# Seven block products in place of eight in the third layer's first product, with its weights streamed from DRAM

## Chip, cores and metric

The kernel runs on 1 core of a Trainium2 chip. The metric is device microseconds of one execution. Three runs of the kernel before took 900.82, 898.17 and 900.29 us; the median is 900.29.

## What is computed

A causal linear attention with a decay per head (batch 4, 8 heads, 768 positions, head size 64) gives 3,072 tokens of 512 features. A first MLP (512 to 1,024 to 512) weights h with its softmax and normalizes it between its two products; a second MLP (512 to 2,048 to 512) puts h cos(h) between its own. Three layers are spoken of: attention; the first MLP, whose products are the first and second layer's; and the second MLP, called the third layer here.

```
x = attention(q, k, v)                      # 3072 x 512
h = x @ w_in;  solu = h * softmax(h);  x = layernorm(solu) * g_ln @ w_out
h = x @ w_in2                               # 512 -> 2048
out = (h * cos(h)) @ w_out2                 # 2048 -> 512
```

All weights are given in float64. Every product is made of three float32r passes: high by high, low by high and high by low.

## The kernel before, in words

Nothing is written in program order. `record` (L843) calls methods that hand operations to `Plan` with an engine, a cost, what they read and write, and a due time (the TensorE clock at that point plus a bias). `Plan.order` (L129) then simulates the engines: TensorE takes its list in order (with a small look ahead), the others the ready operation with the lowest due time, SyncE its transfers by due time. The order found is what is issued, so on the chip each engine works through a fixed list.

**Up to about 120 us**: w_in and w_out are turned from float64 words into float32 halves, and attention (`attn`, L337) runs five steps of 128 tokens ahead of the first layer (`mm1`, L513, then `norm`, L535).

**From 120 to 320 us**: the loop of `record` runs the last 14 steps of `mm1` and 19 of the 24 units of the second layer (`mm2`, L606: one block of 512 tokens by 128 features, 24 matmuls, y stored to DRAM) behind their transposes (`transp`, L584). Beside each unit one `keep` (L482) is handed over, 16 in all: `words` (L400) loads 1 MB of w_in2 or w_out2 as raw words (one ScalarE operation L410, four VectorE operations L414 to L430), and the float32 values go back to DRAM. Keeps alternate between two raw tiles and two word tiles.

**The seam, 320 to 384 us**: the last held unit (HOLD = 1), the transposes and `mm2` of block 5, and the first four columns of the third layer's block 0. `load_kept` (L491) brings each kept piece back once, splits it into halves on ScalarE (L502) and VectorE (L506), and leaves all of w_in2 and w_out2 in SBUF. `load_y` (L638) brings y back and splits it.

**The third layer, 384 us to the end**: for each of 6 blocks of 512 tokens, 16 columns. `up` (L714) makes one 128x512 tile of h with 12 matmuls of 128x512 (L728), over all four slices of the depth. The wave behind it is eight operations: reduction of the angle (L733 on ScalarE, L738, L742 and L746 on VectorE), sine (L749, ScalarE), product (L752, VectorE), high half (L756, ScalarE) and low half (L760, VectorE). `down` (L777) makes 12 matmuls (L789) of a finished column, three columns later, into four accumulators, which are copied and stored at the end of the block.

Of the kernel before, what the change touches and what calls it, by code (L numbers as in the profile page):

```python
# [35 lines left out]
LAG = 3  # L36
EARLY = 5
HOLD = 1
NU = 10
RING = 5  # L40
# [12 lines left out]
SHARE = 0.7  # L53
# [5 lines left out]
LAND = 2.0  # L59
LOOK = 10  # L60
# [9 lines left out]
B_YS = 6.0  # L70
B_LOAD = 4.0
B_LOW = 4.0
JOIN = 2
PARTS = ((0,), (1,), (2, 3), (0, 1), (0, 1, 2, 3))
# [23 lines left out]
class Plan:  # L98
# [30 lines left out]
    def order(self):  # L129
# [18 lines left out]
        at, sat, out, owed = 0, 0, [], 0.0  # L148
# [4 lines left out]
        while len(out) < n:  # L153
            best = None
            for e in engines:
# [6 lines left out]
                elif e == "SP":  # L162
                    while sat < len(sp) and done[sp[sat]]:
                        sat += 1
                    if sat == len(sp):
                        continue
                    cand = [i for i in sp[sat:sat + 8 + stuck] if not left[i] and not done[i]
                            and (stuck or ops[i][7] <= ops[sp[sat]][7] + SP_WIN)]
                else:
                    cand = avail[e]  # L170
# [19 lines left out]
            if e == "POOL" and ops[i][6] == "big":  # L190
                if free["DVE"] > start:
                    free["DVE"] += SHARE
                else:
                    owed = end
            if e == "DVE" and start < owed:
                end += SHARE
                owed = 0.0
# [18 lines left out]
class Body:  # L216
# [21 lines left out]
    def shut(self, name):  # L238
# [4 lines left out]
            "ltl": "lt", "o1h": "o1", "o1l": "o1", "yh": "sb", "yl": "sb", "gh": "sb",  # L243
            "gl": "sb", "h2": "psh", "acc": "psacc", "o": "wo"}

    def add(self, eng, cost, fn, r=(), w=(), **k):
        pools = set()
        for key in (*r, *w):
            if key[0] in ("raw", "wt"):
                pools.add(key[1])  # L250
            elif key[0] == "h":
                pools.add(("ps1", "psb")[key[1]])
            elif key[0] in self.home:
                pools.add(self.home[key[0]])
# [132 lines left out]
    def split(self, n):  # L387
# [9 lines left out]
        self.add("DVE", 0.70, low, r=[("x", n % RING), ("xh", n % 2)], w=[("xl", n % 2)])  # L397


    def words(self, key, src, pool, slot, apart, wide=2, late=0.0):  # L400
# [3 lines left out]
        def fetch():  # L404
            raw = self.new(pool, ("raw", key), [128, wide, 512, 2], I32, f"raw{slot}")
            self.nc.sync.dma_start(out=raw, in_=src)

        def top():
            t = self.new(pool, ("wt", key), [128, wide, 512], I32, f"wt{slot % 2}")
# [26 lines left out]
        self.add("SP", 0.5, fetch, r=[("pool", pool)], w=[rk], mb=0.5245 * wide, bias=b)  # L436
        self.add("ACT", 0.1 + 0.53 * wide, top, r=[rk], w=[wk], bias=b)
        self.add("DVE", 0.17 + 0.28 * wide, clamp, w=[wk], bias=b)
        self.add("DVE", 0.17 + 0.28 * wide, shift, w=[wk], bias=b)
        self.add("DVE", 0.15 + 0.55 * wide, sign, r=[rk], w=[wk], bias=b)  # L440
        self.add("DVE", 0.15 + 0.55 * wide, low, r=[wk] if apart else [rk], w=[rk] if apart else [wk], bias=b + late)
# [5 lines left out]
    def w1(self, c, k, wide, slot):  # L447
# [4 lines left out]
        ks = slice(k, k + wide)  # L452

        def high():
            self.nc.scalar.activation(out=self.w1h[:, ks, cs], in_=self.t["head", key], func=AF.Copy)

        def low():
            self.nc.vector.tensor_tensor(out=self.w1l[:, ks, cs], in0=self.t["full", key],
                                         in1=self.w1h[:, ks, cs].bitcast(F32), op=ALU.subtract)
# [3 lines left out]
                 bias=self.bias + B_LOW)  # L463

    def o1(self, e, pool, slot):
        key = ("o1", e)
        rk, wk = self.words(key, self.pair("w_out1", 2 * e, slice(0, 1024)), pool, slot, True)
        for i in range(2):
# [11 lines left out]
            self.add("DVE", 0.75, low, r=[rk, ("o1h", j)], w=[("o1l", j)], bias=self.bias)  # L480

    def keep(self, what, src, slot):  # L482
        rk, wk = self.words(what, src, "stg", slot, False)

        def store():
            t = self.p["dram"].tile([128, 2, 512], F32, name="kept_%s_%d_%d" % what)
            self.t["kept", what] = t
            self.nc.sync.dma_start(out=t, in_=self.t["full", what])
        self.add("SP", 0.4, store, r=[wk], w=[("kept", what)], mb=0.524, bias=self.bias + B_STORE)

    def load_kept(self, what, dst, keys, pools):  # L491

        sl = self.used["kt"] = self.used.get("kt", -1) + 1
        sl %= 2

        def fetch():
            t = self.new("stg", ("back", what), [128, 2, 512], F32, f"wt{sl}")
            self.nc.sync.dma_start(out=t, in_=self.t["kept", what])

        def high():  # L500
            hi, lo = dst()
            self.nc.scalar.activation(out=hi, in_=self.t["back", what], func=AF.Copy)  # L502

        def low():
            hi, lo = dst(False)
            self.nc.vector.tensor_tensor(out=lo, in0=self.t["back", what], in1=hi.bitcast(F32), op=ALU.subtract)  # L506
        wk = ("wt", "stg", sl)
        self.add("SP", 0.4, fetch, r=[("kept", what)], w=[wk], mb=0.524, bias=-12.0)
        self.add("ACT", 1.10, high, r=[wk] + [("pool", p) for p in pools], w=keys, bias=B_BACK)
        self.add("DVE", 1.25, low, r=[wk], w=keys, bias=B_BACK)  # L510


    def mm1(self, n, c, parts=((0, 1, 2, 3),), passes=(0, 3), look=1, done=True):  # L513
# [4 lines left out]
        for ks in parts:  # L518
            def go(ks=ks):
# [4 lines left out]
                for k in ks:  # L524
                    for m, (a, w) in list(enumerate(((xh, self.w1h), (xl, self.w1h), (xh, self.w1l))))[slice(*passes)]:
                        self.nc.tensor.matmul(out=h[:, c], lhsT=a[:, k], rhs=w[:, k, cs], start=(k + m == 0),  # L526
# [79 lines left out]
    def mm2(self, g, d, look=1):  # L606
        ds = slice(d * 128, (d + 1) * 128)
        pool = "ps1" if g == NBLK - 1 and d % 2 else "pst"
        yk = [("y1",)] if pool == "pst" else [("h", 0, 0), ("h", 0, 1)]
        for f in range(4):  # L610
# [14 lines left out]

        def copy():
# [11 lines left out]
    def load_y(self, n):  # L638
        for k in range(KD):
            def fetch(k=k):  # L640
                self.t["yt", n, k] = t = self.t["yts"][:, k]
                self.nc.sync.dma_start(out=t, in_=self.t["y1d", n][:, k])

            def high(k=k):
                if k == 0:
                    self.new("sb", ("yh", n), [128, KD, 512], F32R, "yh")
                    self.new("sb", ("yl", n), [128, KD, 512], F32R, "yl")
                self.nc.scalar.activation(out=self.t["yh", n][:, k], in_=self.t["yt", n, k], func=AF.Copy)

            def low(k=k):  # L650
                self.nc.vector.tensor_tensor(out=self.t["yl", n][:, k], in0=self.t["yt", n, k],
                                             in1=self.t["yh", n][:, k].bitcast(F32), op=ALU.subtract)
            self.add("SP", 0.4, fetch, r=[("y1d", n, k)], w=[("yt", k)], mb=0.262, bias=-15.0)
            self.add("ACT", 0.65, high, r=[("yt", k)], w=[("yh", k)] + ([("yh", i) for i in range(1, KD)] if k == 0 else []))
            self.add("DVE", 0.70, low, r=[("yt", k), ("yh", k)], w=[("yl", k)])

    def w2(self, c, e):
        what = ("in", c, e)
        ks = slice(2 * e, 2 * e + 2)
        T = self.t  # L660
        if c == 0:
            i, j = self.used["u"], self.used["u"] + 1
            self.used["u"] += 2
            keys = [("u", i % NU), ("u", j % NU)]

            def dst(fresh=True):
                if fresh:
# [392 lines left out]
```

## Time and profile before

| | |
|---|---|
| median of 3 runs | 900.29 us |
| the profiled execution | 902.23 us, span 900.2 us |
| granted TensorE clock, mean | 0.993 |
| TensorE / VectorE / ScalarE busy | 98 / 64 / 46% |
| HBM read, written | 68.2 MB, 21.0 MB |

The span is the time from the first to the last instruction; about 2 us of the execution lie around it. Durations are those of one profiled execution. Matmuls are pipelined, so one lasts longer in a row than the distance to the next; that distance is read from the chain of waits, where a run of matmuls stands with its length and count.

### The profile page before, as it was taken

How to read it: one execution, taken by the hardware profiler on the slowest of the kernel's cores; microseconds unless marked ns; L12 is line 12 of the kernel's file. 1: busy time of each engine (PE TensorE's matmuls, PEld its weight loads, DVE VectorE, ACT ScalarE, POOL GpSimd, SP SyncE). 2: the span in 40 equal slices, each digit the busy share in tenths (PEclk: the TensorE clock that was granted, in tenths of full speed). 3: DMA queues.
4: the chain of work that ended last, by engine and by line, in shares of the span. 5: the costliest groups of instructions: out<-in, count | busy, mean ns of one | idle time of the engine just before them, and what ended most of it. 6: DMA issues, size and time to landing. Idle time of an engine off the chain costs nothing.

```text
span 900.2 us, 15838 instructions
## 1 busy us (share of the span) xinstructions
PE 879.1 (98%) x6648; PEld 728.1 (81%) x6648; DVE 577.6 (64%) x849; ACT 417.0 (46%) x658; POOL 93.1 (10%) x193
## 2 busy tenths in 40 slices
PE   7899999999999999999999999999999999999997
PEld 6688888888788877878888888888888888888886
DVE  6778786867676674466566566656665565557553
ACT  4677674635445475344343343434433443334332
POOL 0134431322422220000000000000000000000000
PEclk8999999999999999999999999999999999999999
DMA  9754727666663643241030003000300030001002
GB/s 351 256 179 146 266 90 256 219 248 239 213 216 135 194 169 94 82 137 40 1 93 1 1 1 94 0 1 1 94 0 1 1 94 1 0 17 31 1 0 48
DMA packets 29031, 90.21 MB, mean 100 GB/s; under 512 B 3360, under 2 KB 3360, under 8 KB 28960
## 3 DMA queue, kind: packets, MB, share of 16 engines
q1 hardware_dynamic: 28816, 89.14, 29.9%
q8 instruction: 52, 0.85, 0.4%
q14 instruction: 19, 0.16, 0.1%
q10 hardware_dynamic: 144, 0.06, 0.0%
HBM read 68.22 MB, written 20.97 MB: 99 GB/s over the span
## 4 chain that ended last, share of the span: by engine, by line
PE 85%; DMA 7%; DVE 2%; ACT 2%; issue 2%; POOL 1%; SPq 1%; ACTq 0%; DVEq 0%; POOLq 0%
PE acc L789 29%; PE h L728 29%; PE h L526 11%; PE y L620 8%; DMA raw<-w_out_dram 2%; PE sc L313 2%; PE tr L588 2%; DMA raw<-w_in_dram 2%; DMA dk<-kq_dram 2%; PE S L321 1%; PE h L620 1%; PE y L334 1%; DMA sv<-vk_dram 1%; DMA yts<-y1d 1%; DVE wt L423 1%
## 5 line engine op out<-in xcount | busy, mean ns | idle before, releaser
L789 PE MATMUL acc<-o2h,gh 128*128 128x512 f32 x384 | 149.5, 389 | 0.7 <-ACT ys L628 0.7
L728 PE MATMUL h<-yh,w2h 128*128 128x512 f32 x384 | 149.8, 390 | 0.0
L728 PE MATMUL h<-yl,w2h 128*128 128x512 f32 x384 | 149.4, 389 | 0.0
L789 PE MATMUL acc<-o2l,gh 128*128 128x512 f32 x384 | 149.4, 389 | 0.0
L728 PE MATMUL h<-yh,w2l 128*128 128x512 f32 x384 | 149.4, 389 | 0.0
L789 PE MATMUL acc<-o2h,gl 128*128 128x512 f32 x384 | 149.4, 389 | 0.0
L749 ACT ACTIVATE kr<-kr,hp 128x512 f32<-128x512 f32 x96 | 69.4, 723 | 151.2 <-DVE kr L746 151.2
L752 DVE TENSOR_TENSOR kr<-kr,h 128x512 f32<-128x512 f32 x96 | 65.9, 686 | 62.3 <-ACT kr L749 62.3
L738 DVE SCALAR_TENSOR_TENSOR kr<-kr,h 128x512 f32<-128x512 int32 x96 | 65.8, 686 | 59.7 <-ACT kr L733 59.7
L760 DVE TENSOR_TENSOR gl<-kr,gh 128x512 fp32r<-128x512 f32 x96 | 66.3, 691 | 52.5 <-ACT gh L756 52.5
L733 ACT ACTIVATE kr<-h 128x512 int32<-128x512 f32 x96 | 57.2, 596 | 79.9 <-PE h L728 79.8
L756 ACT ACTIVATE gh<-kr 128x512 fp32r<-128x512 f32 x96 | 60.6, 631 | 61.5 <-DVE kr L752 61.4
L789 PEld LDWEIGHTS acc<-o2h,gh 128*128 128x128 f32 x384 | 72.1, 188 | 16.1 <-ACT ys L628 1.2
L728 PEld LDWEIGHTS h<-yl,w2h 128*128 128x128 f32 x384 | 72.1, 188 | 15.0
L789 PEld LDWEIGHTS acc<-o2l,gh 128*128 128x128 f32 x384 | 72.1, 188 | 15.0
L728 PEld LDWEIGHTS h<-yh,w2l 128*128 128x128 f32 x384 | 72.1, 188 | 14.9
L789 PEld LDWEIGHTS acc<-o2h,gl 128*128 128x128 f32 x384 | 72.1, 188 | 14.9
L728 PEld LDWEIGHTS h<-yh,w2h 128*128 128x128 f32 x384 | 72.0, 188 | 14.8
L526 PE MATMUL h<-w1h,xh 128*128 128x512 f32 x192 | 79.1, 412 | 1.7 <-ACT xh L390 1.7
L526 PE MATMUL h<-w1h,xl 128*128 128x512 f32 x192 | 76.2, 397 | 0.6 <-DVE xl L394 0.6
L526 PE MATMUL h<-w1l,xh 128*128 128x512 f32 x192 | 74.2, 394 | 0.1
L620 PE MATMUL y<-lth,o1h 128*128 128x512 f32 x176 | 69.9, 397 | 3.1 <-ACT ys L628 3.1
(82 smaller groups left out, 1388.3 us busy)
## 6 DMA issues: line engine op xcount, KB each, us to landing
sv<-vk_dram SPq DMA_DIRECT2D x24, 640.0 KB, 6.4
dk<-kq_dram SPq DMA_DIRECT2D x24, 512.0 KB, 6.1
raw<-w_out_dram SPq DMA_DIRECT2D x12, 1024.0 KB, 7.2
raw<-w_in_dram SPq DMA_DIRECT2D x11, 1024.0 KB, 10.0
y1d<-ys SPq DMA_DIRECT2D x24, 256.0 KB, 3.0
yts<-y1d SPq DMA_DIRECT2D x24, 256.0 KB, 4.2
out_dram<-o SPq DMA_DIRECT2D x48, 128.0 KB, 2.3
kept_in<-wt SPq DMA_DIRECT2D x8, 512.0 KB, 3.0
```

The lines of the kernel that those rows point to most:

```text
L313: self.nc.tensor.matmul(out=sc[r, j], lhsT=dk[r, 0, j], rhs=dk[r, 1, j], start=True, stop=True)
L526: self.nc.tensor.matmul(out=h[:, c], lhsT=a[:, k], rhs=w[:, k, cs], start=(k + m == 0), stop=(k == KD - 1 and m == 2))
L588: self.nc.tensor.transpose(out=tr[:, t * 128:(t + 1) * 128], in_=self.t["u", 4 * g + t].rearrange("p c f -> p (c f)")[:, j * 128:(j + 1) * ...
L620: self.nc.tensor.matmul(out=self.t["y1", g, d], lhsT=w[:, j, ds], rhs=a, start=(j + m == 0), stop=(j == K1 - 1 and m == 2))
L728: nc.tensor.matmul(out=h, lhsT=w[:, cs], rhs=a[:, k], start=(m == 0), stop=(m == 3 * KD - 1))
L733: nc.scalar.activation(out=T["ki", n, j], in_=T["h2", n, j], func=AF.Identity, scale=INV2PI, bias=0.25)
L738: nc.vector.scalar_tensor_tensor(out=r, in0=ki, scalar=-C1, in1=T["h2", n, j], op0=ALU.mult, op1=ALU.add)
L749: nc.scalar.activation(out=T["r", n, j], in_=T["r", n, j], func=AF.Sin, bias=self.hp[:, 0:1])
L752: nc.vector.tensor_tensor(out=T["r", n, j], in0=T["r", n, j], in1=T["h2", n, j], op=ALU.mult)
L756: nc.scalar.activation(out=T["gh", n, j], in_=T["r", n, j], func=AF.Copy)
L760: nc.vector.tensor_tensor(out=T["gl", n, j], in0=T["r", n, j], in1=T["gh", n, j].bitcast(F32), op=ALU.subtract)
L789: nc.tensor.matmul(out=T["acc", n, t], lhsT=a[:, ts_], rhs=w, start=(j == 0 and m == 0), stop=(j == K2 - 1 and m == 2))
```

## The change

The first product of the third layer takes 1,024 tokens (two blocks) at a time, a super-block, of which there are three. An iteration makes 256 columns of h for both blocks: a product of two by two blocks (halves of the columns, halves of the depth, the two token blocks). It is done with seven block products instead of eight, each of 6 matmuls (two slices of the depth, three passes), on sums and differences of the blocks.

- The sums and differences of w_in2 (seven slots, each as high and low half) are made in `keep`, beside the words, and stored in DRAM (`cbd`); w_out2's two halves likewise (`o2d`). There is one raw tile, one word tile and one tile `big`, through which all 16 pieces pass.
- The third layer streams them: `load_cb` brings the 1.84 MB of an iteration into one of three buffers, three iterations ahead, and `load_o2` 1.05 MB into one of three. Buffer 0 of the first is the tile `big`. The split of whole weights (`load_kept`) is gone.
- `load_y` makes the sums and differences of y for two blocks, with halves, in tiles where w_in's halves and attention's tiles stood. Half of it for the first super-block is made in the loop of the middle stage (at step 21), half after it.
- The products accumulate in banks X (two, alternating), W and Z. X is copied by ScalarE after products 1, 6 and 7, while it goes on accumulating; VectorE adds the copies to W or Z. The tiles from 2 and 4 belong to the first block of the two (near), those from 7 and 3 to the second (far).
- In the first half of a super-block the near tiles go through `parts` (what `down` was), three matmuls at a time, between the products. The far tiles wait in SBUF as finished products; in the second half their halves are made and their `parts` run, with no products beside them.
- The seam has the products of iteration 0 between the transposes and the last second-layer units; HOLD is 2, and RING, the ring of attention outputs, 4.
- The planner counts GpSimd's large operations and VectorE's operations with two inputs in SBUF as excluding each other.

```
 NBLK = NT // 512
-LAG = 3
+NSUP = NT // 1024
 EARLY = 5
-HOLD = 1
+HOLD = 2
 NU = 10
...
+ORDER = (("1", 0), ("5", 0), ("6", 0), ("2", 0), ("7", 2), ("4", 3), ("3", 3))
+SEAM = ("t:0 t:1 P:1 P:2 t:2 t:3 P:5 t:4 t:5 P:6 m:0:0:1 t:6 t:7 P:7 m:0:1:3 P:4 m:0:3:4 P:3"
+        " m:1:0:4 m:2:0:4 m:3:0:4")
...
@@ keep @@
+        rk, wk = self.words(what, src, "stg", 0, False, early=EARLIER)
...
+        def part(m, i, n, ca, cd, src):
+            self.add("ACT", ca, high(i, n, src), r=[wk], w=[("big", m)] + ([] if m else [("big",), ("big", 1), ("big", 2)]), bias=b)
+            self.add("DVE", cd, low(i, n, src), r=[wk], w=[("big", m)], bias=b, name="two")
+
+        part(0, 0, 2, 0.62, 0.70, lambda: top2(0))
+        part(1, 2, 1, 0.38, 0.42, lambda: quarter(1, 1))
+        mix((1, 1), (0, 1), (1, 1), ALU.add)
+        mix((0, 1), (0, 0), (0, 1), ALU.subtract)
+        mix((0, 0), (1, 1), (0, 0), ALU.subtract)
+        mix((1, 0), (1, 0), (0, 0), ALU.subtract)
+        part(2, 3, 4, 1.10, 1.25, sums)
...
+                self.nc.sync.dma_start(out=T["cbd", it][:, e], in_=T["qs", what][:, i].bitcast(F32))
+            self.add("SP", 0.4, store, r=[("big",)] + [("big", m) for m in range(3)], w=[("cbd", 2 * c + i, e)], mb=0.459, bias=b + B_STORE)
...
@@ load_cb, product, parts @@
+        it, sl = q % 8, q % 3
...
+        old = {0: [("big",), ("big", 0), ("big", 1), ("big", 2)], 1: [("u", k) for k in range(4)], 2: []}[sl] if q < 3 else []
+        if sl != 1:
+            self.add("SP", 0.5, fetch, r=r, w=[("cb", sl)] + old, mb=1.835, bias=B_CB)
...
+    prods = {"1": ("X", 0, 0, True), "5": ("Z", 6, 3, True), "2": ("W", 1, 1, True), "6": ("X", 3, 6, False),
+             "7": ("X", 4, 5, False), "4": ("X", 2, 4, False), "3": ("Z", 5, 2, False)}
...
+            out = T[key]
             m = 0
+            for e in range(2):
+                w, y = T["cb", q % 3][e], T["Y", e]
+                for i, j in ((0, 0), (1, 0), (0, 1)):
+                    nc.tensor.matmul(out=out, lhsT=w[i][:, a], rhs=y[b][:, j], start=(start and m == 0), stop=(m == 5),
+                                     skip_group_check=True)
                     m += 1
+        need = [(k, e) for k in (("Yb",) if b < 3 else ("Yt",)) for e in range(2)]
+        need += [(k, e, {0: 0, 1: 0, 2: 2, 3: 3, 4: 3, 5: 5, 6: 5}[b]) for k, e in need]
+        self.add("PE", 1.36, go, r=need + [("cb", q % 3)], w=[key], name=f"P{which} {q}", ni=12)
...
+            i = {"1": 1, "6": 2, "7": 3}[which]
+            self.add("ACT", 0.62, copy(i), r=[key], w=[("yt", 0, i)], bias=B_POST)
+        if which == "2":
+            self.add("DVE", 0.70, plus(("yt", 0, 1), 1, ("W",)), r=[("W",)], w=[("yt", 0, 1)], bias=B_POST)
+            self.wave(q, ("yt", 0, 1), None, True)
+        if which == "7":
+            self.add("DVE", 0.70, plus(("hs", 2 * it + 1), 3, ("Z",)), r=[("yt", 0, 3), ("Z",)], w=[("hs", 2 * it + 1)], bias=B_POST)
+            self.wave(q, ("hs", 2 * it + 1), None, False)
+        if which == "4":
+            self.wave(q, key, None, True)
+        if which == "3":
+            self.add("DVE", 0.70, plus(("hs", 2 * it), 2, ("Z",)), r=[("yt", 0, 2), ("Z",)], w=[("hs", 2 * it)], bias=B_POST)
+            self.wave(q, ("hs", 2 * it), None, False)
+
...
+                    if j == 1 and t == 3 and k + 3 < 16 * NSUP:
+                        self.load_o2(k + 3)
...
@@ record @@
+        nk, todo = 0, []
+        for s in range(NSUP):
+            for it in range(8):
+                q = 8 * s + it
+                if q:
+                    owed = len(todo) - (BEHIND if it else 0)
+                    for p, fill in ORDER:
+                        self.product(q, p)
+                        for _ in range(min(fill, owed)):
+                            owed -= 1
+                            todo.pop(0)()
+                    assert owed == 0
+                if q + 3 < 8 * NSUP and q >= 0:
+                    self.load_cb(q + 3)
+                mine = [gs for gs, i in self.near]
+                self.near = []
+                todo += self.parts(2 * s, nk, mine, it, first=it == 0, last=it == 7)
+                nk += 1
+            if s + 1 < NSUP:
+                self.load_y(s + 1)
+            for it in range(8):
+                two = []
+                for j in range(2):
+                    gs, lk = self.gslot(), ("hs", 2 * it + j)
+                    self.halves(gs, lambda lk=lk: self.t[lk], lk, B_HALF)
+                    two.append(gs)
+                while len(todo) > BEHIND:
+                    todo.pop(0)()
+                todo += self.parts(2 * s + 1, nk, two, it, first=it == 0, last=it == 7)
+                nk += 1
+            while len(todo) > (8 if s + 1 < NSUP else 0):
+                todo.pop(0)()
```

## Rows read from the trace of the kernel before

**Rows 1.** The page's first part: busy us, share and instructions of each engine.

```profile
PE 879.1 (98%) x6648; PEld 728.1 (81%) x6648; DVE 577.6 (64%) x849; ACT 417.0 (46%) x658; POOL 93.1 (10%) x193
```

**Rows 2.** Busy time by stretch: PE, PEld, DVE, ACT, POOL, then clock, DMA share, GB/s.

```profile
0.00:40.00 40.00, 34.15 (x716) 29.35 (x720) 29.48 (x39) 21.35 (x40) 2.01 (x10) 0.91 0.85 308
40.00:120.00 80.00, 75.79 (x1362) 62.96 (x1351) 61.62 (x84) 56.74 (x89) 34.59 (x78) 0.98 0.58 191
120.00:320.00 200.00, 196.28 (x2051) 162.89 (x2051) 139.62 (x175) 103.71 (x157) 50.91 (x96) 1.00 0.59 206
320.00:384.00 64.00, 61.40 (x283) 49.75 (x282) 31.47 (x44) 32.23 (x48) 5.62 (x11) 1.00 0.32 103
384.00:884.00 500.00, 500.00 (x2206) 413.97 (x2207) 309.88 (x502) 199.56 (x320) 0.00 (x0) 1.00 0.10 27
```

**Rows 3.** TensorE's waits from 110 to 400 us: total, times, longest.

```profile
PE y L620 <- ACT ys L628: 3.1, 4, 1.0
PE tr L588 <- DVE ltl L599: 2.5, 4, 0.8
```

**Rows 4.** The chain that ended last: start us, us, what.

```profile
324.92 2.73 PE h L526 x12
...
386.86 2.72 PE h L728 x12
```

**Rows 5.** Timeline, 704 to 711 us: one wave behind its last matmul (start, us).

```profile
704.71 0.39 PE L728 MATMUL h<-yl,w2h 128*128 128x512 f32 x1
...
705.20 0.60 ACT L733 ACTIVATE kr<-h 128x512 int32<-128x512 f32 x1 [0.79 <-PE h L728]
...
705.82 0.69 DVE L738 SCALAR_TENSOR_TENSOR kr<-kr,h 128x512 f32<-128x512 int32 x1 [0.69 <-ACT kr L733]
...
707.27 0.43 DVE L746 TENSOR_SCALAR kr<-kr 128x512 f32<-128x512 f32 x1
...
708.49 0.69 DVE L752 TENSOR_TENSOR kr<-kr,h 128x512 f32<-128x512 f32 x1 [0.79 <-ACT kr L749]
...
709.88 0.69 DVE L760 TENSOR_TENSOR gl<-kr,gh 128x512 fp32r<-128x512 f32 x1 [0.70 <-ACT gh L756]
```

**Rows 6.** Timeline near 340 us: a copy of y and the matmul behind it.

```profile
339.62 0.60 ACT L628 ACTIVATE ys<-y 128x512 f32<-128x512 f32 x1 [1.18 <-PE y L620]
...
340.26 0.50 PE L620 MATMUL y<-lth,o1h 128*128 128x512 f32 x1 [0.69 <-ACT ys L628]
```

**Rows 7.** VectorE by line, 120 to 320 us: the word operations (busy, mean ns).

```profile
L430 DVE SCALAR_TENSOR_TENSOR wt<-raw,wt 128x1024 int32<-128x1024 int32 x16 | 22.4, 1403 | 0.4
...
L423 DVE SCALAR_TENSOR_TENSOR wt<-raw,wt 128x1024 int32<-128x1024 int32 x16 | 20.9, 1309 | 0.4
...
L414 DVE TENSOR_SCALAR wt<-wt 128x1024 f32<-128x1024 f32 x16 | 11.3, 707 | 27.6 <-ACT wt L410 27.6
L418 DVE TENSOR_SCALAR wt<-wt 128x1024 int32<-128x1024 int32 x16 | 11.1, 693 | 0.4
```

**Rows 8.** Groups of the whole span by form: the splits of 128x1024.

```profile
L506 DVE TENSOR_TENSOR w2l<-wt,w2h 128x1024 fp32r<-128x1024 f32 x8 | 9.6, 1220 | 7.2 <-ACT w2h L502 7.2
...
L502 ACT ACTIVATE w2h<-wt 128x1024 fp32r<-128x1024 f32 x8 | 8.4, 1057 | 0.5 <-DMA wt<-kept_in 0.3 <-PE h L526 0.2
```

**Rows 9.** DMA issues of the page: count, KB each, us to landing.

```profile
raw<-w_out_dram SPq DMA_DIRECT2D x12, 1024.0 KB, 7.2
...
kept_in<-wt SPq DMA_DIRECT2D x8, 512.0 KB, 3.0
```

**Rows 10.** Timelines of ScalarE and SyncE: first and last keep, start and store.

```profile
131.82 1.11 ACT L410 ACTIVATE wt<-raw 128x1024 f32<-128x1024 f32 x1
...
138.01 0.33 SPq L488 DMA_DIRECT2D kept_in<-wt  x1
...
302.07 1.12 ACT L410 ACTIVATE wt<-raw 128x1024 f32<-128x1024 f32 x1 [2.87 <-DMA raw<-w_out_dram]
...
308.69 0.32 SPq L488 DMA_DIRECT2D kept_out<-wt  x1
```

More of the change, by code (lines that the diff above doesn't have):

```diff
@@ L166, in order @@
                         continue
-                    cand = [i for i in sp[sat:sat + 8 + stuck] if not left[i] and not done[i]
+                    cand = [i for i in sp[sat:sat + 16 + stuck] if not left[i] and not done[i]
                             and (stuck or ops[i][7] <= ops[sp[sat]][7] + SP_WIN)]
@@ L190, in order @@
             if e == "POOL" and ops[i][6] == "big":
[L191 to L197, printed above, removed]
+                end += max(0.0, held - start)
+                owed = end - 0.14
+            if e == "DVE" and ops[i][6] == "two":
+                end += max(0.0, owed - start)
+                held = end
             free[e] = end - (EASE if e in ("DVE", "ACT") else 0.0)
@@ L479, in o1 @@
             self.add("ACT", 0.72, high, r=[wk, ("pool", "o1")], w=[("o1h", j)], bias=self.bias)
[L480 to L510, printed above, removed]
+            self.add("DVE", 0.75, low, r=[rk, ("o1h", j)], w=[("o1l", j)], bias=self.bias, name="two")
@@ L624, in mm2 @@
                      look=look, name=f"mm2 {g},{d},{f}", ni=12)
+        if 3 not in parts:
+            return
         def copy():
@@ L635, in mm2 @@
         self.add("SP", 0.4, store, r=[("ys",)], w=[("y1d", g, d)], mb=0.262, bias=B_YS)
[L638 to L655, printed above, removed]
@@ new lines, in load_o2, with fetch @@
+    def load_o2(self, k):
+        T, nc = self.t, self.nc
+        it, sl = k % 8, k % 3
+        def fetch(l):
+            if ("o2", sl, l) not in T:
+                T["o2", sl, l] = (self.new("u", ("o2u", l), [128, 2, 512], F32R, f"u{8 + l}", "o2u") if sl == 0
+                                  else self.new("wo", ("o2w", sl, l), [128, 2, 512], F32R, f"o2{sl}{l}"))
+            nc.sync.dma_start(out=T["o2", sl, l].bitcast(F32), in_=T["o2d", it][:, l])
+        for l in range(2):
+            self.add("SP", 0.4, lambda l=l: fetch(l), r=[("o2d", it, l)],
+                     w=[("o2", sl)] + ([("u", 8), ("u", 9)] if k == 0 and l == 0 else []), mb=0.524, bias=B_O2)
@@ new lines, in wave, with gslot, halves, f7 @@
+        self.add("ACT", 0.74, f5, r=[] if first else [("table",)], w=[rk] + ([("table",)] if first else []), bias=b)
+        self.add("DVE", 0.70, f6, r=[hk, rk], w=[gk], bias=b, name="" if hk[0] == "X" else "two")
+        if near:
+            self.halves(gs, r, rk, b)
+    def gslot(self):
+        n = self.used["G"] = self.used.get("G", -1) + 1
+        assert n % 5 not in self.live
+        self.live.add(n % 5)
+        return n % 5
+    def halves(self, gs, g, gk, b):
+        T, nc = self.t, self.nc
+        def f7():
+            nc.scalar.activation(out=T["G", gs][:, 0], in_=g(), func=AF.Copy)
+        def f8():
+            nc.vector.tensor_tensor(out=T["G", gs][:, 1], in0=g(), in1=T["G", gs][:, 0].bitcast(F32), op=ALU.subtract)
+        self.add("ACT", 0.65, f7, r=[gk], w=[("G", gs)], bias=b)
+        self.add("DVE", 0.70, f8, r=[gk], w=[("G", gs)], bias=b, name="two")
@@ L942, in record @@
             attend()
[L944 to L952 removed]
+        self.rooms()
@@ L968, in record @@
-        for d in range(KD):
-            self.mm2(g, d)
-            if d == 1:
-                self.o2(1)
+        for word in SEAM.split():
+            kind, *arg = word.split(":")
+            if kind == "t":
+                self.transp(g, int(arg[0]))
+            elif kind == "P":
+                self.product(0, arg[0])
+            else:
+                d, a, b = (int(i) for i in arg)
+                self.mm2(g, d, range(a, b))
+            if word == "t:7":
+                self.load_cb(1)
+                self.load_o2(0)
```

494 lines of the change are left out of this document (294 added, 200 removed).

## The prediction

> **What bounds the kernel now.** I began with the busy table: TensorE is busy for 98% of the span and VectorE for 64% [rows 1]. The busy time by stretch says where that holds [rows 2]. From 384 us to the tail the third layer runs 500 us without one idle microsecond on TensorE, while VectorE is busy for 310 and ScalarE for 200. From 120 to 320 us (attention, first and second layer, and the turning of w_in2 and w_out2 into words) TensorE idles 3.7 us; from 320 to 384, the seam, 2.6. In both, TensorE's waits are on copies by ScalarE and splits by VectorE [rows 3]. The chain of waits prices a matmul: 12 of 128x512 take 2.72 us, 0.2267 each, group after group without a gap [rows 4].
>
> So a matmul removed from the third layer is worth 0.227 us, as long as VectorE, ScalarE and the transfers keep up with a shorter layer, and as long as the work moved forward doesn't make the middle stage wait.
>
> **The change part by part.**
>
> *The matmuls.* `up` issues 6 blocks x 16 columns x 12 = 1,152 matmuls. The seven products issue 3 x 8 x 7 x 6 = 1,008: they work on half of the depth (two slices of 128 rows, three passes each) and 512 columns as before, so the price is the same. 144 x 0.2267 = **32.6 us less**. The layer becomes 2,160 matmuls, 490 us.
>
> The Trainium skill (TensorE: Matmul & The Clock Gate, Back-to-back issue gap) gives about 131 ns as the sustained spacing of 512-column matmuls. By it the term would be an estimated 18.9 us; the trace disagrees, and the measurement decides.
>
> *VectorE and ScalarE in the third layer.* One wave (reduction, sine, product, two halves) has VectorE operations of 0.69, 0.69, 0.43, 0.69 and 0.69 us [rows 5]. An iteration now makes four 128x512 tiles. In the first half of a super-block (42 matmuls of products, 24 of `parts`, 15.0 us on TensorE) VectorE does 4 x 2.50 for the waves, 2 x 0.69 for the near halves and 3 x 0.69 for the new additions: 13.5 us, 90%. Independent neighbours overlap a little. ScalarE, bounded from the gaps between those rows (0.62, 0.79 and 0.70 for its three operations), needs with three more copies at most 8.9 of 15.0. The second half (24 matmuls an iteration, 43.5 us in all) has 16 far halves (11 us), the splitting of the next Y (14 us), the copies out and what the far waves left over. TensorE stays the bound in both, with a margin of 1.5 us an iteration in the first.
>
> What is new on TensorE's own path is that bank X is copied while it accumulates: product 6 must wait for the copy of X after product 1, 7 for that after 6, and 4 for that after 7. Nothing in the trace reads a bank midway; the nearest rows are the copy of y, which begins 0.49 us after its last matmul begins (as f1 does [rows 5]) and lets TensorE go on 0.64 after that [rows 6]: 1.13 in all. Between the two matmuls lies 0.23 + 1.36 us of another product or two fills, so 0.46 us are left for ScalarE to be late. An operation in its way lasts up to 0.79. Lower bound 0; upper, all 72 copies late by 0.33: 24 us. ScalarE is busy under 60% of the time, and the planner puts these copies first, so I take **+2**, near the low end. Whatever waits there holds every matmul behind it, since TensorE takes its list in order. The other locks have more room: the temporary of product 1 is free 10 us after product 2, and the chain it waits for (addition and wave up to its last product) is about 5 us in [rows 5].
>
> Between super-blocks Y is loaded (2.1 MB, some 5 us), then mixed and split: 14 us of VectorE and 7.6 of ScalarE, 22 if nothing overlapped, under 38 us of `parts`. **+1** for the two of them, bounds 0 and 10.
>
> *Streaming.* A first half moves 1.84 + 1.05 MB per 15.0 us, 192 GB/s. A second half moves 8.4 (w_out2), 2.1 (Y), 1.0 (out) and 1.8 MB (the next w_in2 parts) in 43.5 us: 306 GB/s. The start of the kernel moved 308 at a DMA share of 0.85 [rows 2], that is 362 if full. SyncE issues some 70 transfers per super-block of 163 us, at 0.32 us each. I take 0: each buffer is refilled two iterations ahead, and that is the cover; without it, see the third rival.
>
> *The middle stage.* A keep is now more than words. Words cost VectorE 65.7 us for 16 [rows 7]. Added per w_in2 piece: halves of 0.69, 0.42 and 1.22 and four mixes of 0.42 (0.42 is read between 0.69 at 512 and 1.22 at 1,024 [rows 8]), 4.0 us; per w_out2 piece one half of 1.22. That is 8 x 4.0 + 8 x 1.2 = 42 us more, on 140 of 200: VectorE goes from 70% to 91%. The splits that left the seam (16 of 1.22 on VectorE and 1.06 on ScalarE [rows 8]) were cover, not path. Existing waits on VectorE and ScalarE are 5.6 us [rows 3]. Bounds: 0 if the keeps only fill idle time; +14 if these waits grow as the idle share shrinks, 30 to 9. The keeps' 32 larger stores also join SyncE's list, where one that waits for VectorE holds the loads of attention queued behind it. I take **+4**, nearer the low end because keeps are planned with a later due time than the stage's own work.
>
> The Trainium skill (SBUF — State Buffer, Who interferes with whom) adds that a VectorE instruction with two SBUF inputs and a GpSimd instruction that reads SBUF exclude each other; most of the added ones are such. The trace agrees as far as it goes: these word operations, 1.22 alone, average 1.31 and 1.40. By it the 42 would be an estimated 45.
>
> *The seam.* This is where the change is tightest. Before, keeps alternated between two raw and two word tiles. Now all 16 pass through one raw, one word and one `big` tile, and the same tiles then hold the first w_in2 parts, half of Y and the integers. So product 1 of iteration 0 waits for the last keep, its store (3 us) and a load of 1.8 MB (7.2 us for 1 MB [rows 9]; I take 11). It stands two transposes behind the held units. The first layer ended at 327.65 [rows 4]; with one more second-layer unit (5.44 us) held behind it, at 322. Two held units and two transposes later it is 334. So the last keep must be through by 334 - 11 - 3.5 = 320. Bare of any queueing, words take 1.12 + 0.71 + 0.69 + 1.31 + 1.40 = 5.2 us [rows 7, 10]; a w_in2 piece adds 0.70 + 0.69 + 0.42 + 4 x 0.42 + 1.06 + 1.22 = 5.8, a w_out2 piece 1.06 + 1.22 = 2.3. The 16 chains back to back are 8 x 11.0 + 8 x 7.5 = 148 us, from 131.8 on: a room of 188, 1.27 times the bare chain. Before, a keep took 6.42 us in the mean of 16, from 6.2 in the first to 6.6 in the last [rows 10], against a bare 5.2: 1.23 times. At 1.23 it is 6 us early; at 1.30, with a fuller VectorE, 4 late. I take 1.30: **+4**; bounds -3 (the seam's waits go with the loads) and +20.
>
> *Without cost or gain:* RING 5 to 4 (an x is taken long before its slot returns), the tail (the same last two parts per tile, then copies and store), and the planner's new orders up to 120 us. That stretch idles 10 us on TensorE now [rows 2], so between -3 and +3.
>
> **Sum:** -32.6 + 2 + 1 + 4 + 4 = -21.6. The profiled execution took 902.2 us (span 900.2 and 2.0 around it) and would take 880.6; the median of the runs is 1.9 below it, so 900.3 - 21.6 = **879**.
>
> **The rivals.**
>
> *VectorE becomes the bound of the first halves.* For it: 13.5 of 15.0, orders fixed beforehand, dependent operations 0.73 apart instead of 0.69 [rows 5]. Against it: far waves may slip by an iteration, and the second half has room. It decides from 1.5 us per iteration upward; at 15.75 us an iteration instead of 15.0, 18 us come back beside transitions, middle stage and seam: 900.3 - 32.6 + 18 + 9 = about **895**.
>
> *The keep chain runs late (the slower side).* Place: the last keep's `big` tile, before product 1 of iteration 0. Price: 148 us times the excess of the stretch over 1.27. With the other terms at +7 it eats the whole gain from a stretch of 1.44; at 1.52 it is 37 us late and the kernel takes **912**. For it: VectorE at 91%, a single buffer. Against it: 1.23 measured at 70%, and an overdue keep goes ahead of younger work.
>
> *The stream is too slow.* If the second halves got the 206 GB/s of the middle stage [rows 2], 13.3 MB would take 65 us instead of 43.5: 3 x 21 us, about **942**. Against it: the middle stage did not ask for more, and the start moved 308.
>
> *Each product saves less than it should.* A matmul that begins after a wait lasts 0.50 us instead of 0.39 [rows 5, 6]. If each of the 168 products began so, 18 us would come back, with the same 11 us of costs: about **897**. Against it: groups of 12 follow one another without a gap [rows 4]. By the skill's spacing, named above, the saving alone would shrink, to an estimated 892.
>
> **How the numbers follow.** Forecast 0.76 with a range of its own of 870 to 888; VectorE bound 0.10; keeps late 0.08; stream 0.04; smaller saving 0.02, all of it under 897.6. A measurement of this kernel can tell 0.3%, 2.7 us, from no change. Faster: all of the forecast and the smaller saving, 0.06 of VectorE: 0.84. Same: 0.03 of VectorE, 0.01 of late keeps: 0.04. Slower: the rest, 0.12. The low end is all four costs at zero, 868; the high end takes in the milder half of the VectorE case: 893.
>
> **What would show it.** Right: 2,160 matmuls of 0.227 us in the third layer; TensorE without gaps in the first halves; VectorE near 90% in them and in the middle stage; 2 to 8 us of TensorE waiting in the seam for `cb` or Y. Wrong: rows of TensorE waiting for the X copies that sum to over 10 us, for transfers of `o2` or `cb`, or for the transposes' splits; a last keep after 325 us.

## The result and the profile after

The changed kernel took 911.2 us (median of nine runs, 903.53 to 918.01) against 899.69 for the kernel before (nine runs, 896.15 to 900.89). One of the nine, 918.01 us, counts as a slow run; the ratio, 1.0101 with a 95% interval of 1.0064 to 1.0139, is of the other eight, whose median is 908.4. That is about 1% slower, where 879 and faster had been forecast. The profiled execution is the slowest of those eight, 915.32 us with a span of 913.5, so the losses read from it are some 7 us larger in all than at the median.

The page's busy line (as in [rows 1]) of the kernel after:

```profile
PE 866.0 (95%) x6504; PEld 711.8 (78%) x6504; DVE 643.1 (70%) x993; ACT 467.6 (51%) x746; POOL 89.6 (10%) x193
```

The 144 matmuls are gone (6,648 to 6,504), yet TensorE is busy for only 13.1 us less, though the matmuls that left are 144 x 0.2267 = 32.6. Busy time by stretch, with the columns of [rows 2], kernel after:

```profile
120.00:320.00 200.00, 180.93 (x1923) 148.92 (x1922) 146.35 (x199) 108.15 (x161) 43.18 (x87) 0.94 0.64 227
320.00:420.00 100.00, 93.16 (x428) 75.15 (x427) 63.45 (x91) 50.49 (x76) 10.64 (x21) 0.98 0.57 198
420.00:880.00 460.00, 453.20 (x1978) 372.52 (x1977) 337.14 (x577) 228.48 (x376) 0.00 (x0) 0.99 0.59 204
280.00:300.00 20.00, 12.00 (x159) 10.00 (x157) 8.63 (x12) 6.52 (x9) 3.19 (x5) 0.66 0.72 259
```

From 120 to 320 us TensorE idles 19.1 us (3.7 before), at a mean granted clock of 0.94 (1.00 before). The last row is the worst spot: 8 of 20 us idle and a mean clock of 0.66, so part of the stretch ran at 1.2 GHz and part at 2.4. Over the span the granted clock is 0.974, before 0.993.

The spans add up: 913.5 - 900.2 = 13.3 us, made of **-32.6** (matmuls), **+26.4** (TensorE's idle time, 913.5 - 866.0 = 47.5 against 21.1) and **+19.5** (busy time beyond the matmuls that left: 866.0 against 879.1 - 32.6 = 846.5). The last term goes with the clock: by its mean, 0.026 x 913.5 - 0.007 x 900.2 = 17.5 us more of full speed were not granted. Of the idle time, 15.4 us arose from 120 to 320, 4.2 from 320 to 420, and 6.8 from 420 to 880.

What TensorE waited for in the kernel after: total, times, longest.

```profile
PE sc L325 <- DMA dk<-kq_dram: 13.5, 7, 4.7
PE y L346 <- issue: 7.2, 2, 3.9
PE y L697 <- ACT ys L708: 5.2, 4, 3.1
PE acc L973 <- DMA o<-o2d: 4.8, 2, 2.6
PE tr L665 <- DVE ltl L676: 2.1, 3, 0.9
...
PE acc L973 <- DMA o2u<-o2d: 2.0, 2, 1.1
```

(`sc`, the scores, and `y` at L346 are attention's; `ys` and `ltl` belong to the second layer and its transposes; `o` and `o2u` are tiles with parts of w_out2.) The first row is attention's load of its keys (`dk`, by `load` at L292), a part that the change doesn't touch. In the kernel before it was one wait, near the start:

```profile
PE sc L313 <- DMA dk<-kq_dram: 1.1, 1, 1.1
```

From 120 to 320 us, 12.6 us in six waits are for `dk` after, and none before. The second row is two gaps in which TensorE waited for nothing that the profile shows; one of 3.9 us near the start, with one of 4.1 in the kernel before, and a new one of 3.3 at 290 us, which is part of the 8 idle microseconds of the worst spot; what makes it is not shown. SyncE's timeline of the kernel after shows what the loads of `dk` stand behind:

```profile
185.75 0.42 SPq L713 DMA_DIRECT2D y1d<-ys  x1
191.30 0.80 SPq L586 DMA_DIRECT2D cbd<-big  x2
192.19 0.88 SPq L292 DMA_DIRECT2D dk<-kq_dram  x1
...
209.36 0.80 SPq L586 DMA_DIRECT2D cbd<-big  x2
210.26 0.88 SPq L292 DMA_DIRECT2D dk<-kq_dram  x1
```

SyncE issues nothing from 186.2 to 191.3. Its next entry, the store of a keep (two transfers), waits for VectorE; once it has gone, the load goes within 0.1 us. The same order stands at 262.6 and 278.7. The chain that ended last runs through it (start us, us, what; kernel after):

```profile
190.14 1.14 DVE big L568
...
191.30 0.32 SPq L586
...
192.19 7.42 DMA dk<-kq_dram
...
199.66 0.33 PE sc L325 x3
```

VectorE's last low half of a keep (`big`, L568) releases the store; the store lets the load through; the load releases TensorE. No data of the keep is needed by attention: only SyncE's list joins them.

**Theory.** The planner (`Plan.order`) takes SyncE's transfers by due time, and one may only be chosen if it is due at most `SP_WIN` = 10 us after the oldest still open. VectorE's added work makes the keeps' stores late; attention's loads stand behind them, and since SyncE issues in the order of its list (as in the timeline above), TensorE runs dry, and then runs at a lower clock for a while. **Rivals:** the stream loads the DMA engines so that every load lands late; or VectorE is simply too full, whatever the order.

### The profile page after: what moved, and what is told of

It reads as the page before. It is cut to its first block, busy times and chain, and to the rows that moved or that the text cites. A ratio compares the mean times of both kernels' runs of the same rounds, so it can differ in the third digit from the quotient of the medians.

```text
span 913.5 us, 15993 instructions
## 1 busy us (share of the span) xinstructions
PE 866.0 (95%) x6504; PEld 711.8 (78%) x6504; DVE 643.1 (70%) x993; ACT 467.6 (51%) x746; POOL 89.6 (10%) x193
## 4 chain that ended last, share of the span: by engine, by line
PE 74%; DMA 12%; DVE 6%; ACT 3%; issue 2%; POOL 1%; SPq 1%; ACTq 0%; DVEq 0%; POOLq 0%
PE acc L973 26%; PE X L867 14%; PE h L603 10%; PE Z L867 7%; DMA dk<-kq_dram 6%; PE y L697 5%; PE W L867 3%; PE y L346 2%; DMA o<-o2d 2%; PE sc L325 2%; PE h L697 2%; PE S L333 1%; PE tr L665 1%; DVE sm L621 1%; DVE big L568 1%
## 5 line engine op out<-in xcount | busy, mean ns | idle before, releaser
L973 PE MATMUL acc<-o,G 128*128 128x512 f32 x768 | 187.6, 395 | 4.8 <-DMA o<-o2d 4.8
L973 PEld LDWEIGHTS acc<-o,G 128*128 128x128 f32 x768 | 146.2, 191 | 37.0 <-DMA o<-o2d 5.6
L603 PE MATMUL h<-w,xh 128*128 128x512 f32 x384 | 131.9, 411 | 3.9 <-ACT xh L402 2.0
L973 PE MATMUL acc<-o2u,G 128*128 128x512 f32 x384 | 93.7, 390 | 2.0 <-DMA o2u<-o2d 2.0
L603 PEld LDWEIGHTS h<-w,xh 128*128 128x128 f32 x384 | 75.1, 196 | 22.5 <-ACT xh L402 2.2
L973 PEld LDWEIGHTS acc<-o2u,G 128*128 128x128 f32 x384 | 71.9, 188 | 17.7 <-DMA o2u<-o2d 2.8
L603 PE MATMUL h<-w,xl 128*128 128x512 f32 x192 | 78.1, 407 | 0.6 <-DVE xl L406 0.6
L927 ACT ACTIVATE rs<-rs,hp 128x512 f32<-128x512 f32 x96 | 68.8, 718 | 15.7 <-DVE rs L924 15.3
L955 DVE TENSOR_TENSOR G<-hs,G 128x512 fp32r<-128x512 f32 x48 | 32.6, 692 | 51.2 <-ACT G L952 51.1
L697 PE MATMUL y<-ltl,o1h 128*128 128x512 f32 x168 | 66.5, 396 | 0.4 <-DVE ltl L676 0.4
L697 PE MATMUL y<-lth,o1l 128*128 128x512 f32 x168 | 66.3, 395 | 0.0
L325 PEld LDWEIGHTS sc<-dk 64*64 64x64 f32 x768 | 27.3, 146 | 22.2 <-issue 13.3
```

Of the source, the lines that this page charges most:

```text
L325: self.nc.tensor.matmul(out=sc[r, j], lhsT=dk[r, 0, j], rhs=dk[r, 1, j], start=True, stop=True)
L603: self.nc.tensor.matmul(out=h[:, c], lhsT=a[:, k], rhs=self.w1s[k // 2][:, l, k % 2, cs], start=(k + m == 0), stop=(k == KD - 1 and m == 2))
L697: self.nc.tensor.matmul(out=self.t["y1", g, d], lhsT=w[:, j, ds], rhs=a, start=(j + m == 0), stop=(j == K1 - 1 and m == 2))
L927: nc.scalar.activation(out=r(), in_=r(), func=AF.Sin, bias=self.hp[:, 0:1])
L955: nc.vector.tensor_tensor(out=T["G", gs][:, 1], in0=g(), in1=T["G", gs][:, 0].bitcast(F32), op=ALU.subtract)
L973: nc.tensor.matmul(out=T["acc", n, t], lhsT=a[:, ts_], rhs=w, start=(first and j == 0 and m == 0), stop=(last and j == 1 and m == 2))
```

## The experiments

**1. The order of SyncE's list alone.** The planner's finished order is edited: each of attention's loads moves ahead of the pair of keep stores that it stood behind. Operations, waits and the other engines' lists stay.

```diff
+    def ahead(self, out, mine, over, most):
...
     def run(self):
-        for i in self.order():
+        out = self.order()
+        for pair in (('Body.load.', 'Body.keep.', 2),):
+            self.ahead(out, *pair)
+        for i in out:
             self.ops[i][2]()
```

`ahead` moves each of SyncE's entries of the first kind ahead of up to `most` entries of the second, but not past another of the first kind. The kernels with it have their lines 20 further down.

> The changed kernel with the lists of TensorE, VectorE, ScalarE and GpSimd untouched; only on SyncE's list the loads of attention's inputs (dk, sv) go ahead of the pair of keep stores they stood behind. Theory (SyncE's list: a store that waits for VectorE holds the loads behind it): the 13.5 us of TensorE waiting for dk fall below 3, most of the half-clock stretches between 167 and 311 us go with them, and the time falls by 15 to 28 us, to 883 to 896. Rival 1 (the loads land late because the stores load the DMA engines): the loads still land late, waits and time stay within 5 us of 911. Rival 2 (VectorE's 42 us of added work is the limit of the stage): the dk waits go, but waits on VectorE's results take their place, and the time stays over 903.

Measured: 893.41 us (890.65 to 895.65) against 898.18, ratio 0.9933 [0.9910, 0.9957]: against the change's 1.0101 that is 15 us gained, the low edge of what was expected. Its window and TensorE's waits:

```profile
120.00:320.00 200.00, 192.83 (x2013) 158.65 (x2012) 164.80 (x226) 117.91 (x176) 48.77 (x95) 0.99 0.70 248
```

```profile
PE tr L685 <- DVE ltl L696: 5.2, 6, 2.0
PE y L717 <- ACT ys L728: 4.7, 4, 2.4
PE acc L993 <- DMA o<-o2d: 3.9, 2, 2.7
...
PE acc L993 <- DMA o2u<-o2d: 3.0, 2, 1.5
...
PE sc L345 <- DMA dk<-kq_dram: 1.3, 1, 1.3
```

The waits for `dk` fall from 13.5 us to 1.3 and the clock of the stretch comes back to 0.99, with the same work on every engine and more bytes per second in the stretch than after (248 against 227 GB/s). SyncE's timeline of this kernel:

```profile
180.36 0.38 SPq L312 DMA_DIRECT2D dk<-kq_dram  x1
...
185.46 0.80 SPq L606 DMA_DIRECT2D cbd<-big  x2
```

The load goes 5.1 us before the store instead of 0.9 behind it. By spans, 913.5 to 888.9: 13.4 us less idle and 11.2 us less busy (these profiles are the slowest of the one kernel's eight runs and the fastest of the other's; the medians differ by 15 us, not 24.6). That speaks against DMA engines that are too full, and rules out too much VectorE work as the whole of it. But a load that goes first also has no stores beside it while it lands; run 3 separates that.

**2. The loads of w_out2 ahead of the results' stores.** At each block's end eight stores of `out` stand in SyncE's list ahead of loads of w_out2's parts (`load_o2`). The edit is that of run 1 with `('Body.load_o2.', 'Body.leave.', 8)`; `leave` stores the results. Timeline of SyncE, kernel after:

```profile
863.00 5.95 SPq L1003 DMA_DIRECT2D out_dram<-o  x8
869.05 0.54 SPq L808 DMA_DIRECT2D o2u<-o2d  x1
```

> The changed kernel with only SyncE's list altered in the third layer: loads of w_out2's pieces go ahead of the stores of the result they stood behind. Theory (the same mechanism at the block boundaries): TensorE's 6.8 us of waits for o2 fall below 1, the two half-clock stretches at 553 and 717 us go, and the time falls by 5 to 11 us, to 900 to 906. Rival (the stream is too slow for the second halves): the waits stay, time within 3 us of 911.

Measured: 906.51 us (906.12 to 909.62), 1.0092 [1.0063, 1.0120]; the waits for `o` and `o2u` 3.5 + 2.2 us instead of 4.8 + 2.0. A miss: 900 to 906 was expected, and the ratio lies within the interval of the change's 1.0101. The loads pass stores, but not one another, and the waits hardly change. So this run leaves open what they come from; run 5 goes on with it.

> Both moves on SyncE's list together. Theory: the two gains add, 20 to 36 us below 911, 875 to 891, that is 1 to 3% faster than the kernel before; what stays over 868 is the seam's waits and the start. Rivals: within 5 us of 911 (transfers), or 895 to 905 (VectorE).

Measured, with both moves: 892.4 us (888.19 to 897.49), 0.9935 [0.9910, 0.9960]. No more than the first move alone, and outside the 875 to 891 that was expected; the waits for `o` and `o2u` stay at 3.1 + 2.6 us.

**3. VectorE's added work away.** Left out: the four mixes of each w_in2 piece and all low halves but the first piece's; the tile `big` is taken once and not anew for each piece. Loads, stores and ScalarE's work stay. Once with the moved lists and once with the lists of the kernel after. One of the edits:

```diff
         def mix(to, x, y, op):
             def go():
-                self.nc.vector.tensor_tensor(out=quarter(*to), in0=quarter(*x), in1=quarter(*y), op=op)
+                pass
```

> As x_both, but the keeps leave out VectorE's added work (the four mixes of each w_in2 piece and all low halves but those of the first piece, 39 us of VectorE); the stores and loads move the same bytes. This takes the work away with its place in the lists. Theory (VectorE's work matters only through the late stores): at most 5 us faster than x_both. Rival 2 (VectorE's added work limits the middle stage and the seam by itself): 8 us or more faster than x_both, with the gain between 120 and 420 us.

Measured: 887.6 us (886.74 to 890.92), 0.9878 [0.9847, 0.9909].

> The changed kernel with every list as it is, but the keeps leave out VectorE's added work (four mixes of each w_in2 piece, all low halves but the first piece's: 39 us). If the loads of attention are late only because the stores ahead of them wait for VectorE, the stores go earlier and TensorE's waits for dk shrink from 13.5 us by a half or more, without any move on SyncE's list: time 893 to 903. If the late loads come from the transfers themselves, the waits and the time stay (908 to 914).

Measured: 892.53 us (891.02 to 893.88), 0.9929 [0.9902, 0.9955]; the waits for `dk`:

```profile
PE sc L325 <- DMA dk<-kq_dram: 2.0, 4, 0.8
```

With the order of the kernel after untouched, about 16 us go with VectorE's work (908.4 to 892.5); with the loads ahead the same work is worth 892.4 - 887.6 = 4.8. So neither this order nor this work costs much alone: the loss is the work reaching TensorE through the list. This run also separates the hold from the landing. The load at 198.53 us, right behind its pair of stores, took 7.2 us to land, where the one at 210.26 of the kernel after took 7.5; it lands as late behind the same stores, but it was issued in time, and TensorE hardly waits.

**4. The planner's own rule.** Instead of an edit behind the planner, its window for SyncE is widened.

```diff
-SP_WIN = 10.0
+SP_WIN = 40.0
```

> The changed kernel with one constant of the planner: SyncE's choice may look 40 us instead of 10 beyond the due time of its oldest open transfer. In the plan a load of dk then stands 24 to 36 us ahead of its use instead of 5 to 6. All lists are new, so the whole may shift by 5 us either way. Theory: TensorE's waits for dk vanish, time like x_att or a few us lower, 883 to 895. Rival 2 (VectorE in the middle stage): no better than 895 to 903.

Measured: 888.36 us (884.28 to 891.61) against 899.29, 0.9887 [0.9856, 0.9918]; granted clock 0.992 over the span. Its wait for `dk`:

```profile
PE sc L325 <- DMA dk<-kq_dram: 0.8, 1, 0.8
```

This one number undoes the loss. It makes all lists anew, so other shifts may take part; from 160 to 320 us two loads of keys (at 187.21 and 195.99 us) still stand right behind a pair of keep stores, where five do in the kernel after. As far as one run with new lists can show it, the window is what had put the loads there.

**5. The results' stores on another queue.** To the loads ahead, `out` is stored from GpSimd's queue; GpSimd is idle in the third layer.

```diff
-                nc.sync.dma_start(out=self.a["out"][row:row + C], in_=T["o", n, t][b * C:(b + 1) * C])
+                nc.gpsimd.dma_start(out=self.a["out"][row:row + C], in_=T["o", n, t][b * C:(b + 1) * C])
```

> x_att with the stores of the result issued from GpSimd's queue, which has nothing to do in the third layer, at the same places in the order. If the waits for w_out2's pieces come from the stores of the result ahead of them on SyncE's list: the 6.9 us of TensorE waiting for o2 in x_att fall below 2 and the time by 5 to 9 us from 893, to 884 to 888. If they come from slow landing among the other transfers (8.4 us for 512 KB at the first boundary): they stay above 4 us, time within 3 us of 893.

Measured: 891.4 us (890.02 to 893.24), 0.9918 [0.9896, 0.9940]; 884 to 888 was not reached. The waits for `o` and `o2u` fall from 6.9 us in run 1 to 1.4 + 1.5 = 2.9, so the list was part of them, but the time hardly moves (0.9933 to 0.9918, the intervals overlap); the waits for `ltl` and `ys` stay (10.6 us, 9.9 in run 1), and the stores land later. Landing times of the 48 stores of `out_dram`, in the kernel after and then in this one:

```profile
DMA to landing us min/median/max: 2.2/3.1/6.9
```

```profile
DMA to landing us min/median/max: 2.2/5.3/7.7
```

**6. Both together,** the wide window, the moved loads and GpSimd's stores:

> Both: the planner's wider choice for SyncE, attention's loads ahead of keep stores where any are left, and the result's stores on GpSimd's queue. Theory: the gains add to 876 to 888, at least 1% faster than the kernel before. Rival 2: not under 890.

Measured: 886.84 us (883.83 to 888.85), 0.9864 [0.9838, 0.9890], against 888.36 for the window alone: the intervals overlap. And the same without VectorE's added work:

> e_win40_pool without VectorE's added work in the keeps (39 us left out). With the loads ahead of the stores, that work should cost what the prediction took for it, about 4 us with the seam up to 8: 879 to 885. If VectorE's added work is still the limit of the stage: under 877. If it hides wholly: within 2 us of 887.

Measured: 884.87 us (882.54 to 888.05), 0.9848 [0.9814, 0.9882]. With the loads far ahead, that work is worth 2 us, less than the intervals tell apart.

**7. The mechanism in the kernel before.** The reverse edit there: five of attention's loads of keys and one of values go behind the keep store that followed them. Nothing of the change is in this kernel.

```diff
...
+            at = [p for p in range(k + 1, user) if ops[out[p]][2].__qualname__ == "Body.keep.<locals>.store"]
+            if at:
+                out.insert(at[0], out.pop(k))
...
```

> The kernel before, with nothing of the change; only on SyncE's list six loads of attention's inputs (five dk, one sv) go behind the next store of a keep, as they stand in the changed kernel. Theory: that alone makes TensorE wait for dk, about 10 to 20 us in all (a load lands in 6 us and its user comes 0 to 5 us after the store), with the half clock behind the longer waits: 908 to 925 us, the loss of the changed kernel's middle stage without its VectorE work or its transfers. Rival (late loads do harm only together with a full VectorE or with fuller transfers): 899 to 903.

Measured: 919.8 us (917.33 to 921.78) against 900.1, 1.0223 [1.0193, 1.0253]: 20 us from six places in a list. Its window, its first wait (16.6 us, 1.1 in the kernel before), and its chain:

```profile
120.00:320.00 200.00, 184.59 (x1960) 155.35 (x1959) 126.54 (x155) 92.04 (x135) 45.99 (x85) 0.96 0.54 191
```

```profile
PE sc L320 <- DMA dk<-kq_dram: 16.6, 4, 6.1
```

```profile
273.37 1.24 DVE wt L437
274.62 0.33 SPq L495
...
275.04 4.18 DMA dk<-kq_dram
...
279.27 0.37 PE sc L320 x2
```

The same chain as in the kernel after: VectorE's last operation of a keep, its store, the load, TensorE. By spans the 17.3 us are 13.3 idle and 4.0 busy.

**8. A version that keeps the gain.** The kernel of 6, but the last block's results go out from SyncE again, so that the tail has no slower landings, and the planner counts the doubled size of a `cbd` store.

```diff
-...w=[("cbd", 2 * c + i, e)], mb=0.459, bias=b + B_STORE)
+...w=[("cbd", 2 * c + i, e)], mb=0.917, bias=b + B_STORE)
...
-                nc.gpsimd.dma_start(...)
+                (nc.gpsimd if n < NBLK - 1 else nc.sync).dma_start(...)
```

> e_win40_pool with the last block's stores of the result back on SyncE's queue (GpSimd's took longer to land) and the planner counting the 0.92 MB of each cbd store in full. 2 to 4 us from the tail, the rest a new order: 882 to 888, 1.2 to 2% faster than the kernel before.

Measured: 879.48 us (877.37 to 882.69) against 900.1, 0.9781 [0.9755, 0.9807]: 2.2% faster than the kernel before and 3.2% below the change (0.9781 against 1.0101), and faster than the 882 to 888 that was expected. Its windows and waits:

```profile
120.00:320.00 200.00, 195.36 (x2035) 161.72 (x2035) 159.48 (x219) 120.60 (x178) 50.90 (x99) 1.00 0.68 242
320.00:420.00 100.00, 93.72 (x426) 76.11 (x425) 62.62 (x96) 48.26 (x76) 3.72 (x7) 0.98 0.62 214
420.00:870.00 450.00, 444.98 (x1957) 366.44 (x1956) 317.56 (x541) 216.01 (x356) 20.87 (x40) 1.00 0.57 199
```

```profile
PE tr L685 <- DVE ltl L696: 4.4, 4, 1.6
PE y L717 <- ACT ys L728: 3.4, 3, 2.0
PE acc L993 <- DMA o<-o2d: 2.6, 2, 2.2
...
PE acc L993 <- DMA o2u<-o2d: 2.1, 2, 1.3
```

By spans, 880.0 - 900.2 = -20.2: -32.6 + 9.8 idle + 2.6 busy. From 120 to 320 us TensorE idles 4.6 us, 0.9 more than before. HOLD, RING and ScalarE's added work are still those of the change, so they are not the loss in this stage.

> f_2 without its second edit: the last block's stores are on SyncE's queue again, the planner counts 0.46 MB for a cbd store as in the changed kernel. If f_2's gain over e_win40_pool is the tail: 880 to 884. If it is the order that the full size gives: 885 to 888.

The same without the planner's size: 882.61 us (880.81 to 885.68), 0.9816 [0.9787, 0.9846]. About 4 of the 7.4 us between 6 and this version would be the tail and some 3 the new order, but the intervals overlap.

## Why the prediction was wrong

**The matmuls (-32.6): right.** 144 fewer, at the same price. Chain of the kernel after:

```profile
424.79 1.36 PE X L867 x6
426.15 1.36 PE acc L973 x6
```

Six take 1.36 us, 0.2267 each. The fourth rival, a smaller saving, falls, and with it the spacing of 131 ns that the Trainium skill gives (TensorE: Matmul & The Clock Gate, Back-to-back issue gap).

**The copies of X (+2): nothing.** No row of the waits names them; the one wait of a product, 0.7 us, is for `ys`.

**The first halves of a super-block: right.** From 420 to 520 us TensorE has no gap, and none from 546 to 695 and from 740 to 858, which hold the other two first halves. VectorE is at 82% from 420 to 520 (76 to 92% in its parts), where 90% had been forecast. The rival with VectorE as the bound falls too.

**Streaming 0 and transitions +1: 6.8 us.** It stands at the boundaries of blocks, not where I looked. "Each buffer is refilled two iterations ahead, and that is the cover" fails there: eight result stores stand ahead of the loads in SyncE's list. No matmul waited for a load of Y or `cb`. Moving the stores to another queue took 4.0 us of waiting off run 1; what the rest is (the landing of 6 to 8 us there, or accumulators copied late on a busy VectorE) stays open.

**The middle stage (+4): the step that failed.** I wrote that the keeps' stores "also join SyncE's list, where one that waits for VectorE holds the loads of attention queued behind it", and still took a value near the low end "because keeps are planned with a later due time than the stage's own work". That reason is wrong: the due time puts a store late in the list, but the window of 10 us then kept the loads from going past an open one. The sum and its upper bound of 14 were sized by TensorE's waits on VectorE and ScalarE growing, and those didn't grow: the waits for `ltl` and `ys` from 120 to 320 us were 3.7 us before and are 3.0 after. What came in their place was the hold in SyncE's list, which the same paragraph names and gives no price: 12.6 us of waiting for `dk` out of 15.4 us of added idle time, with a granted clock of 0.94 on top. Runs 1 and 4 remove it by the order of lists, run 3 by the work behind the stores, and run 7 makes it in the kernel before.

**A term that was not in the sum: the clock.** Of 45.9 us of added idle and busy time, 19.5 are busy time. The prediction priced a gap on TensorE at its length, though [rows 2] have clocks of 0.91 and 0.98 in the two stretches where TensorE idled most.

**VectorE at 91% in the middle stage: not as put.** It reached 73%, in a stage that TensorE's delays stretched, and 80% in run 8; in both, keeps slip past 320 us, and their work with them. The work itself costs at most 2 to 5 us once the loads are ahead (runs 3 and 6).

**The seam (+4): 4.2 us of idle, by other causes.** The waits are for `ys` (3.8 us) and `ltl`, of the second layer's units, and for the first layer's `u`, and not for `cb` or Y. The last keep's store went at 365.15 us, far past my 325, with the first layer's end itself late at 349.5 instead of 322; product 1 began at 380.50, after a load of `cb` that was issued at 370.13, and no wait of TensorE for it is in the rows. In run 8 the last keep's store went at 336.43, product 1 began at 362.42, and again nothing waited for `cb`. So the keep chain did run late, as that rival said, but TensorE did not wait for it: that the rival's 912 us is next to the measured 911.2 is chance. The stream was not the cause either: `dk` landed in 6.2 us (median) after and 6.1 before.

**How near the sum comes with the list in order.** Run 1, the loads of attention moved and nothing else, gains about 5 us on the kernel before, not 21.6. Run 8 gains 900.1 - 879.48 = 20.6, but with three further edits that the forecast did not have, and its parts are not all those of the sum. Where the forecast adds 3 us in the third layer, 4 in the middle stage, 4 in the seam and nothing for the clock, run 8 has 5.0, 0.9, 3.7 and 2.6. That the totals agree so closely is in part luck.

## What to carry to other kernels

Where an engine works a list in order, as SyncE does here, read for each load what stands ahead of it and whom that waits for: a store that waits for a busy engine turns that engine's lateness into a wait of everyone behind it, with no data in common. When work is added to an engine with idle time, check the lists of its consumers and not only its share; give loads with a near user a place ahead of stores that nobody needs soon, or widen the planner's window so that it can. Price a gap on TensorE above its length.

## What was not expected of the hardware

Short stalls cost more here than themselves: 26.4 us of added idle time came with 19.5 us of slower matmuls, and in the row of 280 to 300 us, where TensorE had stood idle for 8 of 20 us, the mean granted clock is 0.66. How much more differs: in run 7 the surcharge was smaller, 4.0 us on 13.3.

A load issued right behind a keep's stores can also land later: 7.42 us on the chain above, where the median of `dk` is 4.7 us in run 1 and 4.9 in run 8. So part of the length of those waits was the landing, though run 3 shows that without the hold it hardly costs anything. In run 7, behind a store of 512 KB where the keeps of the change store two of 896, it was 4.18.

Stores of 128 KB issued from GpSimd's queue landed in 5.3 us (median, run 5) against 3.4 from SyncE's in run 1, whose kernel differs in nothing else. Whether the queue itself does it, or the loads that no longer wait behind the stores and now run beside them, no run separates.
